# First tiles' masks on VectorE instead of bias products, zero products on TensorE, and a new written order, in a fused attention and tanh-shrink kernel

## The chip, the cores and the metric

The kernel runs on one core of a Trainium2 chip, in one launch. The metric is device time in microseconds. Five engines work side by side, each through its own queue in order: PE (TensorE, matrix products), ACT (ScalarE), DVE (VectorE), POOL (GpSimd) and SP (SyncE, here only DMAs). Three of them also issue DMAs; 16 DMA engines carry them out.

## What is computed

Attention with a few global keys and a local window, and then two matrix products with h - tanh(h) between them. B = 4, H = 8, S = 768, D = 64; 8 global keys, a window of 96; d_model 512, d_ff 2048.

```python
scores = scale * np.matmul(q, k.transpose(0, 1, 3, 2))
rel = pos[:, None] - pos[None, :]
is_global = pos[None, :] < n_global
is_local = (rel >= 0) & (rel < n_local)
keep = is_global | is_local
dist = np.where(is_global & ~is_local, n_local, np.abs(rel))
scores = np.where(keep, scores - slopes[:, None, None] * dist, -1e9)
a = softmax(scores)
x = np.matmul(a, v)      # heads side by side: 3072 rows of 512
h = x @ w_in
out = (h - np.tanh(h)) @ w_out
```

## The kernel before

The 3072 rows are 24 tiles of 128 query rows. `turn_of` puts the four tiles that begin a sequence first; these are tiles 0 to 3 in the kernel's own numbering. A tile has one block of 128 keys if it begins a sequence, and two otherwise (its own keys and those of the tile before, with the 8 global keys copied over the head of the older block where needed).

Every step has a short name, and the order in which the steps are put into the engines' queues is written out by hand in a string, `ORDER`. A second string, `HOMES`, says which buffer or which of the 8 PSUM banks each tile uses. An engine takes its own steps from `ORDER` one after the other; a step that has to wait holds up all that stands behind it on that engine. The steps of tile u:

- `lq.u`, `lk.u`, `lv.u`: loads of q, k and v. For tiles 0 to 2, q and k come as float32, q by ACT's queue and k by SP's (L294). From tile 3 on all loads are issued by POOL and converted on the way (L294 for tiles 3 and 4, L297 later), as are the weights `in.0` to `in.4` (parts of w_in, L300), `out.0` to `out.3` (quarters of w_out, L303) and most stores `st` (L454).
- `cq.u`, `ck.u`: conversion of the float32 rows to bf16, for tiles 0 to 2 (`/a` on ACT, `/d` on DVE).
- `T.u`: transposes. Up to tile 6 on PE (L317 for tiles 0 to 2, L321 for 3 and 4, L312 for 5 and 6), k first and then q; `Te.u.1` (k) and `Te.u.0` (q) copy them out of PSUM (L229 is ACT's copy, L231 DVE's). From tile 7 on, T is a DMA transpose on SP.
- `S.n`: products of keys and queries (L352). `E.u.o`: exponential on ACT (L359). `M.u.o`: the result times a mask on DVE (L363). `AV.u`: products with v and a column of ones (L378). `R.u`: reciprocal and division on DVE (L386, L387). `X.u`, `Xe.u`: transpose of x and its copy (L398).
- `m1.g.f`, `th.g.f`, `g.g.f`: the product with w_in for a group g of tiles (L420), tanh on ACT (L430), h - tanh(h) on DVE (L436). Tiles 0 and 1 are groups of one, tiles 2 to 7 groups of two, the rest groups of four. `m2.u.c.a`: the product with quarter a of w_out (L445), `ev.u` its copy out of PSUM.

The distance bias has two forms. For tile u >= `BIASED` (3 before), the mask `mk[m]` = exp(-slope * distance) is multiplied in after the exponential by step M. For tiles 0 to 2, step `B.u` has PE put the bias into the scores' PSUM banks first, by two products of 128x512 (L275), to which S adds; they have no step M. The masks themselves are made once, from the same kind of products (`bm.m`) and an exponential on ACT (`em.m`). Both rest on constants that DVE derives from `rel`, an iota that POOL makes first of all: `slopes`, `dist`, `first`; `turn` and `ident` are permutation and identity matrices for T and X.

The opening's queues before, as `ORDER` gives them:

```
PE   bm.1 bm.0 B.1 T.1 B.0 T.0 S.1 T.3 B.2 S.0 T.2 S.3 AV.0 S.2 AV.1 X.0 T.4 X.1 AV.2 bm.2 m1.0.0 AV.3 X.2 m1.1.0 X.3
     S.4 m1.2.0 m1.2.6 m1.1.4 ... m2.2.0.0 m1.2.4 m2.1.0.0 m2.0.0.0 m2.2.0.1
DVE  zero ones.0 slopes dist turn first ident ones.1 cq.1 ck.1 ck.0 Te.1.0 Te.0.0 ck.2 Te.3.0 Te.2.0 R.0 R.1 M.3.0 Te.4.1
ACT  lq.1 lq.0 lq.2 table em.1 em.0 cq.0 Te.1.1 Te.0.1 cq.2 E.1.0 Te.3.1 E.0.0 Te.2.1 E.3.0 E.2.0 Xe.0 Xe.1 Te.4.0 em.2
POOL rel lq.3 lk.3 lv.0 lq.4 lk.4 lv.1 lv.2 in.1 in.0 lv.3 in.2 lk.5 lq.5 in.3 out.0 out.1 out.2 lv.4 in.4 lk.6 lq.6
     lv.5 lq.10 lv.6 out.3
SP   lk.1 lk.0 lk.2
```

A function `warm()` with one product of zeros by zeros into bank 7 is there, but the order before does not call it.

Of the kernel before, what the change touches and what calls it, by code (L numbers as in the profile page):

```python
# [17 lines left out]
lq.1 lk.1 zero rel ones.0 lq.0 lk.0 lq.3 slopes lq.2 lk.2 lk.3 dist table lv.0 turn bm.1 first ident lq.4 ones.1 bm.0  # L18
em.1 lk.4 cq.1/d ck.1/d B.1 lv.1 em.0 T.1 lv.2 B.0 cq.0/a ck.0/d in.1 Te.1.0/d Te.1.1/a T.0 in.0 S.1 Te.0.1/a Te.0.0/d
cq.2/a ck.2/d E.1.0 lv.3 T.3 B.2 in.2 Te.3.1/a Te.3.0/d S.0 lk.5 T.2 E.0.0 lq.5 S.3 Te.2.0/d Te.2.1/a AV.0 in.3 R.0  # L20
E.3.0 S.2 AV.1 out.0 X.0 R.1 E.2.0 T.4 out.1 M.3.0 X.1 Xe.0/a AV.2 bm.2 Te.4.1/d Xe.1/a out.2 m1.0.0 R.2 Te.4.0/a em.2
lv.4 AV.3 X.2 R.3 m1.1.0 Xe.2/a X.3 th.0.0 S.4 Xe.3/d th.1.0 in.4 g.0.0 m1.2.0 E.4.0 lk.6 g.1.0 m1.2.6 K.4 E.4.1 M.4.0
lq.6 m1.1.4 th.2.0 M.4.1 m1.2.2 th.1.4 g.2.0 m1.0.4 th.2.6 g.1.4 lv.5 th.2.2 T.5 g.2.6 m1.1.8 th.0.4 Te.5.0/d Te.5.1/a
g.0.4 m1.0.8 th.1.8 g.2.2 lq.10 S.5 th.0.8 g.1.8 m1.2.10 E.5.1 g.0.8 m1.2.8 K.5 th.2.10 M.5.1 m2.2.0.0 lv.6 E.5.0
g.2.10 m1.2.4 th.2.8 M.5.0 m2.1.0.0 g.2.8 th.2.4 m2.0.0.0 g.2.4 out.3 m2.2.0.1 lk.8 m2.2.0.2 m2.0.0.1 AV.4 lq.7
m1.1.12 V.4 lk.10 R.4 m1.2.14 th.1.12 lq.8 m1.0.12 g.1.12 th.2.14 lk.9 g.2.14 m1.2.12 th.0.12 lk.7 m2.1.0.1 g.0.12
th.2.12 lq.9 X.4 g.2.12 AV.5 Xe.4/a m2.1.0.2 R.5 T.6 V.5 lv.7 m2.0.0.2 Te.6.1/a Te.6.0/d lk.11 X.5 m2.2.0.3 Xe.5/a
m2.0.0.3 ev.2.0/a T.10 S.6 ev.0.0/a m1.3.10 T.8 E.6.1 K.6 m1.3.0 E.6.0 M.6.1 T.7 m1.3.2 th.3.10 M.6.0 m2.3.0.0 T.9
th.3.2 g.3.10 m1.3.4 th.3.0 g.3.2 m2.1.0.3 g.3.0 th.3.4 AV.6 g.3.4 ev.1.0/a m1.3.6 R.6 st.1.0 m1.3.12 lv.15 th.3.6 V.6
m2.3.0.1 g.3.6 lq.12 th.3.12 S.7 g.3.12 lv.8 m2.3.0.2 E.7.1 K.7 lv.17 m1.3.8 E.7.0 lk.13 M.7.1 X.6 m2.3.0.3 Xe.6/d  # L30
lv.10 th.3.8 M.7.0 S.8 ev.3.0/a st.0.0 g.3.8 AV.7 lv.9 E.8.1 m1.3.14 V.7 R.7 lq.11 E.8.0 m2.4.0.0 M.8.1 lq.18 X.7
th.3.14 m2.4.0.1 M.8.0 lk.12 Xe.7/a S.9 g.3.14 lq.13 AV.8 E.9.1 K.9 m2.4.0.2 lq.15 R.8 E.9.0 m1.4.6 lv.11 M.9.1 Xe.8
m2.4.0.3 M.9.0 th.4.6 lv.12 T.11 m1.4.8 g.4.6 ev.4.0/a S.10 T.12 th.4.8 AV.9 E.10.1 K.10 g.4.8 m1.4.0 T.13 R.9 E.10.0
m2.5.0.0 M.10.1 Xe.9 m1.4.4 th.4.0 V.9 M.10.0 m1.4.10 th.4.4 g.4.0 m2.5.0.1 th.4.10 g.4.4 AV.10 lq.14 g.4.10 m2.5.0.2
R.10 lv.16 m1.4.2 V.10 lv.13 Xe.10 S.11 th.4.2 lk.15 m2.5.0.3 g.4.2 E.11.0 lk.14 K.11 m1.4.12 K.12 ev.5.0/d E.11.1
st.4.0 m1.4.14 M.11.0 lk.17 th.4.12 M.11.1 m2.6.0.0 th.4.14 st.5.0 g.4.12 m2.6.0.1 E.12.0 g.4.14 AV.11 M.12.0 m2.7.0.0
R.11 m2.7.0.1 V.11 Xe.11 S.12 m2.7.0.2 T.15 E.12.1 m2.7.0.3 E.13.1 M.12.1 T.14 m2.6.0.2 ev.7.0/d E.13.0 AV.12 M.13.1
st.7.0 m2.6.0.3 lq.16 M.13.0 m1.5.7 R.12 ev.6.0/a lv.14 m1.5.6 th.5.7 V.12 Xe.12 lk.16 m1.5.1 g.5.7 th.5.6 lq.17 AV.13
g.5.6 th.5.1 lv.18 m1.5.3 R.13 lq.23 m1.5.0 th.5.3 g.5.1 Xe.13 lk.18 m1.5.11 g.5.3 th.5.0 m1.5.8 g.5.0 lq.19 th.5.11
S.13 g.5.11 lk.19 th.5.8 m1.5.4 g.5.8 E.14.0 T.16 K.14 m1.5.2 K.15 E.14.1 M.14.0 T.17 m1.5.9 th.5.4 M.14.1 m1.5.13  # L40
th.5.2 g.5.4 m1.5.14 E.15.0 g.5.2 m1.5.10 th.5.13 M.15.0 th.5.14 m1.5.5 g.5.13 T.18 th.5.10 g.5.14 m2.8.0.0 th.5.5
g.5.10 m1.5.15 th.5.9 g.5.5 AV.14 th.5.15 g.5.9 m2.8.0.1 T.19 V.14 R.14 m1.5.12 m2.8.0.2 g.5.15 Xe.14 th.5.12 S.14
g.5.12 m2.9.0.0 E.15.1 K.16 m2.8.0.3 E.16.0 M.15.1 m2.9.0.1 ev.8.0/d E.16.1 AV.15 M.16.0 st.8.0 m2.10.0.0 lv.19 R.15
m2.9.0.2 lk.23 V.15 Xe.15 M.16.1 S.15 lv.22 m2.9.0.3 E.17.1 K.17 lv.23 m2.10.0.1 ev.9.0/d E.18.0 st.6.0 m2.10.0.2
M.17.1 lq.22 E.17.0 M.18.0 m2.10.0.3 st.3.0 st.2.0 M.17.0 AV.16 lv.21 m2.11.0.0 V.16 T.23 R.16 lv.20 AV.17 m2.11.0.1
R.17 st.9.0 Xe.16 ev.10.0/a m2.11.0.2 lk.20 V.17 Xe.17 m1.6.0 st.10.0 lq.21 S.16 th.6.0 lq.20 m2.11.0.3 g.6.0 E.19.1
K.19 lk.21 m1.6.9 ev.11.0/d E.19.0 m1.6.6 M.19.1 th.6.9 M.19.0 m1.6.4 th.6.6 g.6.9 m1.6.3 E.18.1 lk.22 g.6.6 m1.6.15
th.6.4 M.18.1 th.6.3 AV.19 g.6.4 AV.18 th.6.15 g.6.3 m1.6.12 R.18 m1.6.2 th.6.12 V.19 Xe.18 m1.6.8 g.6.15 th.6.2 R.19
m1.6.7 th.6.8 g.6.12 Xe.19 m1.6.1 th.6.7 g.6.8 m1.6.11 th.6.1 T.20 g.6.7 m1.6.5 th.6.11 g.6.1 T.21 m1.6.10 g.6.11
th.6.5 g.6.2 m1.6.14 th.6.10 T.22 g.6.5 m1.7.12 th.6.14 g.6.10 m1.6.13 th.7.12 g.6.14 m1.7.1 g.7.12 th.6.13 m1.7.10  # L50
g.6.13 th.7.1 S.17 g.7.1 th.7.10 m2.13.0.0 g.7.10 E.21.0 K.21 m2.12.0.0 K.20 E.20.0 M.21.0 m2.13.0.1 E.20.1 M.20.0
m2.12.0.1 M.20.1 m2.13.0.2 AV.20 m1.7.14 V.20 R.20 m2.13.0.3 th.7.14 Xe.20 m1.7.9 g.7.14 ev.13.0/a m2.12.0.2 th.7.9
m2.12.0.3 g.7.9 S.18 ev.12.0/a m1.7.5 E.21.1 K.22 m2.14.0.0 E.22.0 M.21.1 m1.7.3 th.7.5 M.22.0 m1.7.2 th.7.3 g.7.5
# [13 lines left out]
mk.0:2,3 mk.1:0,1 mk.2:6,7 f32.0.k:3 kq.0:1 f32.0.q:2 f32.1.k:1 kq.1:0 f32.1.q:0 f32.2.k:5 kq.2:3 f32.2.q:4 v.0:0
v.1:1 kq.3:2 v.2:2 kq.4:4 v.3:3 v.4:4 kq.5:0 v.5:5 kq.6:1 v.6:6 kq.7:4 v.7:7 kq.8:3 v.8:9 kq.9:0 v.9:4 kq.10:2 v.10:11
kq.11:1 v.11:5 kq.12:2 v.12:6 kq.13:3 v.13:7 kq.14:1 v.14:9 kq.15:0 v.15:8 kq.16:3 v.16:0 kq.17:2 v.17:10 kq.18:4
v.18:4 kq.19:1 v.19:11 kq.20:2 v.20:7 kq.21:4 v.21:6 kq.22:3 v.22:5 kq.23:0 v.23:1 tr.0.0:1 tr.0.1:7 qk.0:1 s.0.0:2,3  # L70
p.0.0:1 av.0:2,3 x.0:0 xt.0:2 xT.0:0 tr.1.0:6 tr.1.1:0 qk.1:0 s.1.0:4,5 p.1.0:0 av.1:4,5 x.1:1 xt.1:1 xT.1:1 tr.2.0:4
tr.2.1:5 qk.2:3 s.2.0:6,7 p.2.0:3 av.2:4,5 x.2:2 xt.2:3 xT.2:2 tr.3.0:0 tr.3.1:1 qk.3:2 s.3.0:0,1 p.3.0:2 av.3:0,1
x.3:0 xt.3:5 tr.4.0:3 tr.4.1:0 qk.4:4 s.4.0:6,7 s.4.1:0,1 p.4.0:4 p.4.1:1 av.4:0,1 x.4:1 xt.4:0 xT.3:3 tr.5.0:7
tr.5.1:3 qk.5:5 s.5.0:0,1 s.5.1:6,7 p.5.0:3 p.5.1:0 av.5:4,5 x.5:2 xt.5:0 tr.6.0:7 tr.6.1:1 qk.6:6 s.6.0:4,5 s.6.1:0,1
p.6.0:1 p.6.1:2 av.6:4,5 x.6:0 xt.6:3 xT.4:1 qk.7:9 s.7.0:6,7 s.7.1:4,5 p.7.0:0 p.7.1:4 av.7:2,3 x.7:1 xt.7:6 qk.8:8
s.8.0:4,5 s.8.1:6,7 p.8.0:1 p.8.1:3 av.8:6,7 x.8:2 xT.5:0 qk.9:10 s.9.0:2,3 s.9.1:4,5 p.9.0:0 p.9.1:2 av.9:0,1 x.9:0
qk.10:7 s.10.0:6,7 s.10.1:2,3 p.10.0:1 p.10.1:4 av.10:0,1 x.10:1 qk.11:4 p.11.0:3 p.11.1:0 av.11:2,3 x.11:2 qk.12:5
# [30 lines left out]
def kernel(  # L108
# [11 lines left out]
    nc = tc.nc  # L120

    B, H, S, Dh = q.shape
# [15 lines left out]
    R4 = 4  # L138

    ROWS = 5  # L140
    HW = 3
    PE_T = 7
    PE_X = 8
    BIASED = 3
    SINGLE = 2
    NK, NV, NQK = 5, 12, 11
    LAST = [(0, 384), (384, 512)]

    turn_of = sorted(range(NU), key=lambda t: (t % NQ > 0, t))
    nth = [t % NQ for t in turn_of]  # L150
# [438 lines left out]
```

## Time and profile before

| | us |
|---|---|
| median of three runs | 214.47 (213.91 to 216.38) |
| the profiled execution, its own time | 215.35 |
| its span, first to last instruction | 213.5 |
| busy: PE / DVE / ACT / POOL | 204.6 / 130.4 / 120.5 / 76.9 |
| L445, 400 products with w_out | 91.2 |
| L420, 576 products with w_in | 90.5 |
| L275, 12 bias products of 128x512 | 5.4 (mean 587 ns) |
| L359, 44 exponentials of 128x1024 | 43.0 (mean 1023 ns) |
| L363, 41 mask products of 128x1024 | 27.6 (mean 687 ns) |

The span is shorter than the time by what lies around it, 1.85 us. A line of the timeline has the start, the duration, the engine, the line of the code, the operation with what it writes and reads, how many of them are merged, and in brackets the idle time ahead with what ended it. Durations run from start to result; instructions of one engine overlap a little, so the step from one start to the next is often shorter. Twelve bias products are two each for three masks and three tiles.

### The profile page before, as it was taken

The numbers are of one execution on the slowest core, as the hardware profiler recorded it, in microseconds if no ns is written. First come the engines' busy times: TensorE is split into PE (matmuls) and PEld (weight loads), VectorE is DVE, ScalarE is ACT, GpSimd is POOL, SyncE is SP. The second block draws the span as 40 slices with busy tenths as digits, with TensorE's granted clock in tenths as the row PEclk, the third lists the DMA queues.
The fourth block names the chain that finished last, engine by engine and source line by source line (L and its number), as shares of the span: only waits on it lengthen the run. The fifth ranks groups of instructions, "written<-read, shape, count | busy, mean of one in ns | idle before, by whom it ended". The sixth has DMA issues, their size and how long they took to land.

```text
span 213.5 us, 4492 instructions
## 1 busy us (share of the span) xinstructions
PE 204.6 (96%) x1796; PEld 117.2 (55%) x1796; DVE 130.4 (61%) x264; ACT 120.5 (56%) x179; POOL 76.9 (36%) x101
## 2 busy tenths in 40 slices
PE   4799999999999999999999999999999999999994
PEld 1467985857667665544555454444554444444442
DVE  7348883737787975789776498874567435611300
ACT  4579881557678474578445395673853335522422
POOL 8794435730995092780049830000010002002040
PEclk9999999999999999999999999999999999999999
DMA  5999999999999999999919999801021102002136
GB/s 164 243 177 189 208 198 175 179 157 194 128 177 150 141 154 216 181 151 137 175 53 166 195 206 150 147 3 25 0 78 25 25 3 98 0 0 98 52 116 228
DMA packets 100884, 27.55 MB, mean 129 GB/s; under 512 B 91840, under 2 KB 99264, under 8 KB 100864
## 3 DMA queue, kind: packets, MB, share of 16 engines
q0 software_dynamic: 72000, 18.36, 85.1%
q1 hardware_dynamic: 28048, 8.13, 23.5%
q10 hardware_dynamic: 816, 0.79, 1.2%
q8 instruction: 14, 0.23, 0.4%
q14 instruction: 6, 0.05, 0.1%
HBM read 27.26 MB, written 6.29 MB: 157 GB/s over the span
## 4 chain that ended last, share of the span: by engine, by line
PE 68%; issue 12%; DMA 10%; POOL 6%; DVE 1%; ACT 0%; SPq 0%; POOLq 0%; DVEq 0%; ACTq 0%
PE ps L420 30%; PE ps L445 28%; DMA qk<-kq 4%; POOL kq L297 3%; PE ps L352 3%; DMA f<-in_k_dram 3%; PE ps L378 3%; DMA out_dram<-ot 3%; POOL vb L297 2%; PE ps L398 1%; PE ps L317 1%; POOL out_dram L454 1%; PE ps L321 1%; PE ps L275 1%; PE ps L312 0%
## 5 line engine op out<-in xcount | busy, mean ns | idle before, releaser
L445 PE MATMUL ps<-w_out_bf,g 128*128 128x512 bf16 (+2 forms) x400 | 91.2, 371 | 0.0
L420 PE MATMUL ps<-xT,w_in_bf 128*128 128x512 bf16 (+2 forms) x576 | 90.5, 308 | 0.5 <-ACT ot L229 0.5
L436 DVE TENSOR_TENSOR g<-ps,th 128x512 bf16<-128x512 f32 x96 | 65.0, 688 | 38.7 <-ACT th L430 37.5
L430 ACT ACTIVATE th<-ps 128x512 f32<-128x512 f32 x96 | 56.7, 599 | 45.6 <-PE ps L420 44.8
L420 PEld LDWEIGHTS <-w_in_bf 128*128 128x128 bf16 x576 | 50.2, 98 | 33.9 <-issue 0.8
L445 PEld LDWEIGHTS <-g 128*128 128x128 bf16 x400 | 37.0, 98 | 38.0 <-DVE g L436 0.5
L454 POOL DMA_DIRECT2D out_dram<-ot x21 | 12.0, 576 | 106.3 <-ACT ot L229 86.5
L359 ACT ACTIVATE pr<-ps 128x1024 bf16<-128x1024 f32 x44 | 43.0, 1023 | 9.8 <-PE ps L352 9.8
L363 DVE TENSOR_TENSOR pr<-pr,mk 128x1024 bf16<-128x1024 bf16 x41 | 27.6, 687 | 8.0 <-ACT pr L359 7.9
L229 ACT COPY ot<-ps 128x512 f32<-128x512 f32 (+2 forms) x20 | 11.3, 565 | 26.6 <-PE ps L445 19.2
L297 POOL DMA_DIRECT2D vb<-in_v_dram x24 | 21.7, 912 | 5.1 <-DMA w_out_bf<-in_moe_w_out_dram 2.6
L297 POOL DMA_DIRECT2D kq<-in_q_dram x19 | 17.1, 911 | 12.4 <-DMA qk<-kq 8.2
L297 POOL DMA_DIRECT2D kq<-in_k_dram x19 | 17.1, 903 | 1.2 <-PE ps L352 0.5
L387 DVE TENSOR_TENSOR x<-ps,rden 128x512 bf16<-128x512 f32 x24 | 16.6, 692 | 0.8
L378 PEld LDWEIGHTS <-pr 128*128 128x128 bf16 x352 | 13.5, 98 | 4.2 <-issue 0.2
L378 PE MATMUL ps<-vb,pr 128*128 128x65 bf16 x352 | 14.8, 194 | 0.0
L352 PEld LDWEIGHTS <-qk 64*128 64x128 bf16 x352 | 10.2, 96 | 7.0 <-issue 6.3
L352 PE MATMUL ps<-qk 64*128 64x128 bf16 x192 | 10.1, 229 | 0.0
L231 DVE COPY vb<-vb 8x512 bf16<-8x512 bf16 x16 | 5.7, 356 | 5.9 <-PE ps L378 5.9
L275 PE MATMUL ps<-slopes,dist 128*128 128x512 bf16 x12 | 5.4, 587 | 3.1 <-DVE dist L242 3.1
L352 PE MATMUL ps<-qk,qk 64*128 64x128 bf16 x160 | 7.8, 217 | 0.0
L386 DVE RECIPROCAL rden<-ps 128x8 f32<-128x8 f32 x24 | 4.8, 199 | 2.8 <-PE ps L378 2.6
(41 smaller groups left out, 58.8 us busy)
## 6 DMA issues: line engine op xcount, KB each, us to landing
out_dram<-ot POOLq DMA_DIRECT2D x21, 256.0 KB, 2.8
vb<-in_v_dram POOLq DMA_DIRECT2D x24, 128.0 KB, 6.1
kq<-in_q_dram POOLq DMA_DIRECT2D x21, 128.0 KB, 6.9
kq<-in_k_dram POOLq DMA_DIRECT2D x21, 128.0 KB, 7.5
w_out_bf<-in_moe_w_out_dram POOLq DMA_DIRECT2D x4, 512.0 KB, 13.1
w_in_bf<-in_moe_w_in_dram POOLq DMA_DIRECT2D x3, 512.0 KB, 10.5
f<-in_q_dram ACTq DMA_DIRECT2D x3, 256.0 KB, 4.2
f<-in_k_dram SPq DMA_DIRECT2D x3, 256.0 KB, 6.9
```

What stands on the lines that cost most here:

```text
L229: nc.scalar.copy(out=out, in_=in_)
L297: eng(e).dma_start(out=dst, in_=rows_of(src, u).rearrange("h p d -> p h d"))
L352: nc.tensor.matmul(bank(("s", u, o), hh)[:, p * P : (p + 1) * P], buf(("qk", back[u] if o else u))[r, 1, p, :], buf(("qk", u))[r, 0, p, :] ...
L359: nc.scalar.activation(d, banks(("s", u, o), 0, 1), AF.Exp, bias=0.0, scale=scale)
L363: nc.vector.tensor_tensor(out=t, in0=t, in1=mk[:, mask_of(u, o)], op=ALU.mult)
L378: nc.tensor.matmul(t[:, h // (H // 2), h % (H // 2), :], buf(("p", u, o))[:, slot(h), :], buf(("v", back[u] if o else u))[:, h, 0 : Dh + 1 ...
L387: nc.vector.tensor_tensor(out=buf(("x", u)).rearrange("q (a h) d -> q a h d", a=2), in0=t[:, :, :, 0:Dh], in1=rden.to_broadcast([P, 2, H / ...
L420: nc.tensor.matmul(t[:, (f - f0) * n : (f - f0 + 1) * n], w_in_bf[j][:, c, fo : fo + P], x[:, c, 0:n], start=(c == 0), stop=(c == CD - 1),)
L430: nc.scalar.activation(h_view(buf(("th", g, f0)), g, m), h_view(bank(("h", g, f0)), g, m), AF.Tanh, bias=0.0, scale=1.0)
L436: nc.vector.tensor_tensor(out=buf(("g", g))[:, f0 : f0 + m, 0:n], in0=h_view(bank(("h", g, f0)), g, m), in1=h_view(buf(("th", g, f0)), g, ...
L445: nc.tensor.matmul(bank(part)[:, 0 : c1 - c0], buf(("g", g))[:, f, t * P : (t + 1) * P], w_out_bf[f // FJ][:, f % FJ, c0:c1], start=(f == ...
L454: eng(e).dma_start(out=out[turn_of[u] * P : (turn_of[u] + 1) * P, c0:c1], in_=buf(("ot", u))[:, c0:c1])
```

## The change

`BIASED` goes from 3 to 0: steps B.0, B.1 and B.2 with their six products are gone, S starts the sum itself, and tiles 0, 1 and 2 get a step M (M.0.0, M.1.0, M.2.0). The order may hold words `zero:b`, each one product of 128x512 of zeros into bank b; sixteen are in it. `ORDER` and `HOMES` are written anew from end to end.

```diff
-    BIASED = 3
+    BIASED = 0
...
-    def warm():
-        nc.tensor.matmul(ps[:, 7, :], zero[:, 0, :], zero.to_broadcast([P, 4, P]), start=True, stop=True)
+    def warm(b):
+        nc.tensor.matmul(ps[:, b, :], zero[:, 0, :], zero.to_broadcast([P, 4, P]), start=True, stop=True)
...
-            if word == "warm":
-                warm()
+            if word.startswith("zero:"):
+                warm(int(word[5:]))
                 continue
```

The opening's queues after:

```
PE   zero:7 zero:7 zero:7 zero:7 bm.1 bm.0 zero:7 T.1 zero:7 zero:7 T.0 S.1 zero:6 S.0 zero:7 zero:7 T.2 T.3 zero:1 zero:3
     AV.1 S.2 AV.0 S.3 X.1 zero:1 zero:1 zero:1 zero:3 AV.2 X.0 AV.3 bm.2 m1.1.0 X.2 X.3 m1.0.0 m1.2.2 m1.2.4 m1.1.4 m1.2.6
     T.4 m1.2.8 m1.0.4 S.4 m1.2.10 m1.0.12 m1.2.14 m1.2.12 AV.4 T.5 m1.2.0 m1.1.8 m1.1.12 S.5 m2.1.0.0 T.6 m1.0.8 m2.0.0.0
     m2.2.0.0 m2.2.0.1
DVE  zero ones.0 slopes turn dist ident first ones.1 cq.1 ck.1 ck.0 Te.1.1 Te.0.0 cq.2 ck.2 M.1.0 Te.2.1 M.0.0 R.1 R.0
     M.2.0 M.3.0 R.2 R.3 Xe.2 Xe.3
ACT  lq.1 lq.0 lq.2 table em.1 em.0 cq.0 Te.1.0 Te.0.1 E.1.0 E.0.0 Te.2.0 Te.3.0 Te.3.1 E.2.0 E.3.0 Xe.1 Xe.0 em.2 th.1.0
POOL rel lk.3 lq.3 lv.2 lv.1 lv.0 in.0 lv.3 in.1 lq.4 in.2 lk.4 in.3 in.4 lq.5 lk.5 lk.7 lv.4 lq.6 out.0 lk.6 lv.5 out.1
     out.2 out.3
SP   lk.1 lk.0 lk.2
```

The masks' products `bm.0` to `bm.2`, the arithmetic of all other steps and the number of loads and stores are as before.

## The prediction

> **What bounds it now.** I read the page's busy table first, then PE's waits, then the opening.
>
> ```profile
> PE 204.6 (96%) x1796; PEld 117.2 (55%) x1796; DVE 130.4 (61%) x264; ACT 120.5 (56%) x179; POOL 76.9 (36%) x101
> ```
> ```profile
> PE ps L420 <- ACT ot L229: 0.5, 1, 0.5
> ```
>
> The second line is all that PE waited for after 20 us. From there to 210.4 it runs without a gap, so nothing there can get faster by a new order, apart from that 0.5. The page's chain wanders through DMA and POOL between 67 and 119, but PE is full there too. What can shrink is the opening (and the 3.1 us tail, which keeps its shape: last products, two copies, two stores). In windows of 3.41 us (columns: busy PE, weight load, DVE, ACT, POOL, clock, DMA):
>
> ```profile
> 1.77:5.18 3.41, 2.07 (x5) 0.70 (x6) 2.93 (x25) 2.28 (x3) 3.41 (x5) 1.00 0.84 247
> 5.18:8.60 3.42, 2.38 (x12) 1.11 (x10) 0.31 (x2) 1.93 (x4) 2.94 (x5) 1.00 1.19 276
> 8.60:12.01 3.41, 2.72 (x33) 2.19 (x34) 2.12 (x4) 2.39 (x4) 2.31 (x3) 1.00 1.96 177
> 12.01:15.42 3.41, 3.41 (x34) 1.92 (x32) 1.38 (x2) 2.05 (x4) 3.26 (x4) 1.00 1.68 186
> ```
>
> PE's timeline shows the path and a change of speed:
>
> ```profile
> 8.97 1.04 PE L317 MATMUL ps<-turn,kq 128*128 128x128 bf16 x8 [1.42 <-DVE kq L231]
> ...
> 10.87 1.06 PE L321 MATMUL ps<-turn,kq 128*64 128x128 bf16 x16 [0.32 <-DVE qk L231]
> 11.86 1.03 PE L275 MATMUL ps<-slopes,dist 128*128 128x512 bf16 x2
> 12.83 0.61 PE L352 MATMUL ps<-qk 64*128 64x128 bf16 x8
> 13.37 1.03 PE L317 MATMUL ps<-turn,kq 128*128 128x128 bf16 x8
> 14.34 0.61 PE L352 MATMUL ps<-qk 64*128 64x128 bf16 x8
> 14.88 0.62 PE L378 MATMUL ps<-vb,pr 128*128 128x65 bf16 x8
> 15.43 0.40 PE L352 MATMUL ps<-qk 64*128 64x128 bf16 x8
> ...
> 16.92 0.64 PE L321 MATMUL ps<-turn,kq 128*64 128x128 bf16 x16
> 17.49 0.40 PE L398 MATMUL ps<-ident,x 128*128 128x128 bf16 x4
> 17.72 0.41 PE L378 MATMUL ps<-vb,pr 128*128 128x65 bf16 x8
> 17.97 0.59 PE L275 MATMUL ps<-slopes,dist 128*128 128x512 bf16 x2
> ```
>
> T.0 (8.97) starts when DVE has cast tile 0's k, landed at 8.46. The same sixteen products (L321) step on after 0.99 us at 10.87 and 0.57 at 16.92: until about 15.4 PE runs at half speed, though the clock column says 1.00 throughout. PE had worked unbroken for 4.55 us (10.87 to 15.42) when it sped up; the 4.45 us from 3.11 to 7.56 had not brought T.0 to full speed.
>
> **The change, part by part.** *Bias products.* Six of 128x512 go. Four (at 3.11 and 6.50) lie where PE waits for loads: worth nothing, but they were what kept PE busy. B.2's two at 11.86 are on the path: 0.97 us.
>
> *Masks.* M.0.0, M.1.0, M.2.0 come to DVE: 0.60 us of its queue each (M.3.0 at 17.29 to the next at 17.89), and 0.68 plus a hop of 0.05 between E and AV. AV.1 gets this for nothing (PE is at T.2, T.3). Queued behind M.1.0 and M.0.0 are Te.2.1, R.1 and R.0; behind M.2.0, M.3.0 and R.2.
>
> *Turn before dist, ident before first:* dist 0.22 later; bm.1 goes from 3.11 to 3.33. Casts of tile 1 wait for the same DVE queue, T.1 still stands at about 5.5, and everything waits for 8.46 anyway: nothing. (rel leads GpSimd's queue in both, so "distances first" moves nothing here.)
>
> *Zero products.* Sixteen, 0.43 each at half speed (B.2's two take 0.97 with their change-over), 0.22 at full (bm.2: 0.43 for two). Four before bm.1 (about 1.0 to 2.7), one before T.1, two after it: PE is then busy 3.33 to 7.3, 4.0 us, less than the stretch that had no visible effect. Seven lie in idle time. The five from zero:6 to zero:3 lie where PE is on the path or close to it. From T.0 on they leave no gap: by the 4.55 us above, PE is at full speed at 8.97+4.55=13.5.
>
> The Trainium skill, "TensorE: Matmul & The Clock Gate", Part 1, has a free-running window of about 3.4 us that must be busy once. The trace fits that (2.72 busy of 3.41 was not enough, 3.41 was). By this rule the change of speed would fall anywhere from 12.4 to 15.8 (an estimate), or, if a window falls into the 4.0 us, before T.0, and differ between runs; the first lies about my 13.5, the second is the third rival.
>
> *Walk of the new order from T.0,* with each row's duration; loads as before, speed changing at 13.5. PE: T.0 8.97, S.1 9.94, zero to 10.91, S.0 10.91 (12.83 before), two zeros to 12.31 (T.2 could start at 11.55, ck.2 being done: they cost 0.76), T.2 to 13.28, T.3 to 13.96, two zeros to 14.39, AV.1, S.2 14.63, AV.0, S.3 15.28. ACT (0.92 per E, 0.48 per copy): E.1 10.6, E.0 11.56, Te.2.0 13.4, Te.3.0 14.17, Te.3.1 14.65, E.2 15.13, E.3 16.05, Xe.1 16.97, Xe.0 17.45. DVE (0.61 per mask or copy, R 0.23+0.61): M.0.0 13.56, R.1 14.9, R.0 15.74, M.2.0 16.58, M.3.0 to 17.88. PE: X.1 15.88, four zeros to 16.97 (hidden, AV.2 waits for M.2.0), AV.2 17.32, X.0, AV.3 17.93, bm.2, m1.1.0 18.6, X.2, X.3, m1.0.0 19.91, m1.2.2 20.78. Before, m1.2.0 starts at 21.75 with S.4 (0.55) and T.4 (0.57) done, which the new order has yet to do: 20.78+1.12-21.75 = +0.15. B.2's 0.97 and the half-speed time won are spent on zeros ahead of T.2, the masks and ACT, which gets E.2 no sooner than 15.1 (14.98 for E.3 before).
>
> *The queue of loads.* On POOL lv.2, lv.1, lv.0 pass lq.4 and lk.4 (T.4 now comes 4 us into the dense part), in.3 and in.4 pass the w_out parts, and lq.5, lk.5, lk.7, lv.4, lq.6 come ahead of out.0. w_out, then, is later:
>
> ```profile
> 29.84 0.88 POOL L297 DMA_DIRECT2D vb<-in_v_dram  x1 [1.18 <-DMA w_out_bf<-in_moe_w_out_dram]
> ```
>
> Issue n waits for landing n-8 (the ninth waits for the first at 8.5), so this one, the 24th, says that out.1, 16th, landed at 29.8; likewise out.2 32.3, in.4 36.0. Now out.0 is 19th and out.1 22nd. By bytes out.1 then lands at 36.0 (5.0 MB, as much as up to in.4 before); by packet time about 38.7 (the trace's packets last 34 ns at 128 bytes, 60 at 512, 98 at 1,024; over 16 engines a tile of q, k or v, 1,024 packets, is 2.2 us, a w_out part 3.1; out.1 closes 47.4 us of them, in.4 before 41.8 at 36.0, out.3 before 55.9 at 42.9). PE reaches m2.1.0.0 at 20.78+13.9=34.7 (13 m1 of 0.87, 2.6 of S, T, AV) and m2.2.0.1 at 38.6: just covered, so 0. Uncovered it is the second rival.
>
> *The rest of the order.* It has the same products. The 0.5 at 119.5 (a copy that waited for a store) may go, or others come: 0 to -0.5 against some +1; I take 0.
>
> Sum: 215.35 (profiled execution: 213.5 and 1.85 around it) +0.15 = 215.5. The median of the three runs is 0.9 below that execution; as the change of speed may well have come earlier in them, I carry half: **215.1**.
>
> **Rivals.** *The speed changes late (15.4, as before).* The walk with half speed until then has two zeros to 15.13, S.2 15.55, E.3 to 17.95, m1.1.0 19.49, m1.2.2 21.71: +1.08, **216.4**, slower at the edge of what counts. It is also what happens if zero products do nothing for the speed. Against: 4.55 us of unbroken work were enough once.
>
> *w_out late: slower.* If the queue goes on at the 0.71 us per us of packet time that it kept from 20.2 to 36.0, out.1 (5.6 us of packets after in.4's place) lands at about 39.9 and m2.2.0.1 waits 1.3: 215.5+1.3, **216.8**; each further us of landing or a like wait of a later tile adds one. It decides from a landing at 39.7. For: PE never waited for loads here before, with only 1.5 us to spare for in.4 (36.0 against 37.5). Against: the ring is filled sooner.
>
> *Full speed before T.0: faster.* Then T.0 is through at 9.5, E.1 starts 10.0, E.2 13.3, m1.1.0 16.8 (in.1 lands about then), m1.2.2 19.02: -1.6, **213.7**, 213.2 without the 0.5 at 119.5, and 212.3 if the runs lie 0.9 lower as before. For: PE busy from 1.0 with 0.6 us of gap. Against: 4.45 us at the same place did not do it.
>
> **Numbers.** Bounds: 1% is about what runs of this kernel (213.9 to 216.4) can tell; 212.3 and 216.6 are the borders. Forecast 0.40 (within); late speed 0.13 (0.07 slower, 0.06 within); w_out or a like load late 0.25 (slower); early speed 0.22 (0.14 faster, 0.08 within). So faster 0.14, within 0.54, slower 0.32. The range runs from early speed at 212.4 to w_out one us later still, 217.6; the likeliest case alone 214.2 to 216.2.
>
> **What would show it.** L321's sixteen products near 13.3 in about 0.7 us, later ones in 0.57; S.0 at 10.9; PE idle before T.2 none; m1.1.0 at 18.6; no wait of L445 for w_out at 34 to 40; M between E and AV. I am wrong if lk.0 lands elsewhere than 8.5, if T.3 is slow (first rival) or T.0 fast (third), or if PE has gaps after 20 us.

## The result and the profile after

| | before | after |
|---|---|---|
| median of 20 runs each, us | 214.58 (213.32 to 217.17) | 215.68 (213.95 to 217.41) |
| ratio of the times | | 1.0049, 95% interval [1.0027, 1.0071] |
| the profiled execution, its own time | 215.35 | 215.69 |
| its span | 213.5 | 213.4 |
| what lies around the span | 1.85 | 2.29 (median of the 20 runs) |

Medians here and below are of all runs; ratios and their intervals leave out the few runs that were counted as slow.

The change made the kernel slower by half a per cent, which is inside the 1% that was called no difference. The profile after, however, has an opening that is far better than forecast. First, PE's timeline of the opening (start, duration, engine, line, operation, count, idle time ahead and what ended it; line numbers are one higher than before, so L421 is m1, L446 m2, L353 S, L318 and L322 T; L542 is the zero products):

```profile
5.53 0.97 PE L318 MATMUL ps<-turn,kq 128*128 128x128 bf16 x8
6.34 0.59 PE L542 MATMUL ps<-zero 128*128 128x512 bf16 x2
8.04 0.62 PE L318 MATMUL ps<-turn,kq 128*128 128x128 bf16 x8 [1.11 <-DVE kq L232]
...
9.44 0.40 PE L353 MATMUL ps<-qk 64*128 64x128 bf16 x8
9.77 0.61 PE L542 MATMUL ps<-zero 128*128 128x512 bf16 x2
10.21 0.61 PE L318 MATMUL ps<-turn,kq 128*128 128x128 bf16 x8
10.75 0.64 PE L322 MATMUL ps<-turn,kq 128*64 128x128 bf16 x16
...
15.95 1.06 PE L421 MATMUL ps<-xT,w_in_bf 128*128 128x128 bf16 x16
...
17.29 1.93 PE L421 MATMUL ps<-xT,w_in_bf 128*128 128x128 bf16 x24
19.57 1.61 PE L421 MATMUL ps<-xT,w_in_bf 128*128 128x256 bf16 x18 [0.35 <-DMA w_in_bf<-in_moe_w_in_dram]
```

T.0 takes 0.62 us where it took 1.04: PE is at full speed already, from 6.30 on (T.1, which runs across that moment, takes 0.97, the two zeros right behind it 0.59). Tile 0's k also came 1.2 us earlier than in the profile of before (its cast on DVE starts at 7.29, not 8.49; T.0 at 8.04, not 8.97). The first product with w_in is at 15.95. The last eight of the 24 at 17.29 are m1.2.2; they start near 18.18. When the kernel before starts m1.2.0, at 21.75, it has S.4 and T.4 done as well, which take 1.12; with these the new kernel would stand at 19.30. So PE enters the dense part 2.45 us ahead, and yet the span is shorter by 0.1 only. This compares one execution of each kernel: the one of before, at 215.35, lies 0.77 above its median, and half speed lasted until 15.42 in it, so between the medians the lead may well be smaller. The dense part has given nearly all of it back. Its waits, in the list of PE's waits (total, times, longest) of the kernel after:

```profile
PE ps L353 <- DMA qk<-kq: 1.0, 2, 0.6
...
PE ps L421 <- DMA xT<-x: 0.6, 1, 0.6
...
PE ps L421 <- DMA w_in_bf<-in_moe_w_in_dram: 0.3, 1, 0.3
```

Before, the only wait of the dense part was the 0.5 for a copy. All of these are for transfers: a part of w_in, two DMA transposes of q and k, one of x. The timeline shows three of them with the products ahead:

```profile
54.28 0.81 PE L446 MATMUL ps<-w_out_bf,g 128*128 128x512 bf16 x3
55.52 0.40 PE L353 MATMUL ps<-qk 64*128 64x128 bf16 x8 [0.43 <-DMA qk<-kq]
...
85.83 0.81 PE L446 MATMUL ps<-w_out_bf,g 128*128 128x512 bf16 x3
87.29 1.47 PE L421 MATMUL ps<-xT,w_in_bf 128*128 128x512 bf16 x6 [0.65 <-DMA xT<-x]
...
105.65 0.40 PE L353 MATMUL ps<-qk,qk 64*128 64x128 bf16 x8
106.65 0.40 PE L353 MATMUL ps<-qk 64*128 64x128 bf16 x8 [0.60 <-DMA qk<-kq]
```

By the step from one start to the next, less what that step takes without a wait, they cost 0.59, 0.81 and 0.79, and the one for w_in, behind the product that starts at 18.95, costs 0.51: 2.7 in all, against 0.64 before (the 0.5 for a copy). Of 2.45 won, 2.06 are gone by these, and the last product ends 0.17 earlier than before (210.20 against 210.37); some 0.2 are not traced. Then come 0.44 us around the span that before does not have.

What the waits for q and k stand behind shows in the issues of the DMA transposes on SP. The lines give the time an issue takes, minimum, median and largest in ns, the first and last start in us, and the time to landing; first before, from 40 to 57 us, then after:

```profile
L333 SPq DMA_TRANSPOSE qk<-kq x4: 1242/1296/3403, 45.1 to 51.5; - x4
...
DMA to landing us min/median/max: 3.1/4.3/6.1
```
```profile
L334 SPq DMA_TRANSPOSE qk<-kq x3: 2023/2487/2961, 43.2 to 48.5; - x3
...
DMA to landing us min/median/max: 9.0/9.5/10.1
```

They start 2 us earlier, but take 9 to 10 us to land, not 3 to 6: the trace has the three down at 52.2, 55.5 and 58.0, the four of before at 51.1, 52.0, 53.4 and 54.5. In these microseconds POOL issues five loads of q, k and v (41.9 to 47.2), which land up to 58.4; before, it issued none between 43.98 and 54.07, and the last of the earlier ones was down at 50.1. Even there the two transposes issued ahead of that moment took 6.1 and 5.4 us, the two behind it 3.3 and 3.1. So the new order has the transposes and the loads side by side, and what PE needs next is no earlier. That the loads are what slows the transposes is argued from these rows; no run moves the loads alone.

### The profile page after: what moved, and what is told of

It is laid out like the page before. It is cut to its first block, busy times and chain, and to the rows that moved or that the text cites. A ratio compares the mean times of both kernels' runs of the same rounds, so it can differ in the third digit from the quotient of the medians.

```text
span 213.4 us, 4495 instructions
## 1 busy us (share of the span) xinstructions
PE 203.7 (95%) x1780; PEld 116.3 (54%) x1806; DVE 130.4 (61%) x265; ACT 122.1 (57%) x181; POOL 76.9 (36%) x101
## 4 chain that ended last, share of the span: by engine, by line
PE 77%; DMA 19%; issue 1%; POOL 1%; DVE 0%; ACT 0%; POOLq 0%
PE ps L421 34%; PE ps L446 33%; DMA qk<-kq 9%; DMA w_in_bf<-in_moe_w_in_dram 5%; PE ps L353 5%; PE ps L379 4%; DMA kq<-in_q_dram 3%; DMA xT<-x 3%; POOL kq L295 1%; PE ps L313 0%; DVE x L388 0%; PE ps L399 0%; PE ps L322 0%; POOL rel L236 0%; ACT ot L230 0%
## 5 line engine op out<-in xcount | busy, mean ns | idle before, releaser
L421 PE MATMUL ps<-xT,w_in_bf 128*128 128x512 bf16 (+2 forms) x572 | 89.9, 308 | 1.3 <-DMA xT<-x 0.6
L446 PE MATMUL ps<-w_out_bf,g 128*128 128x512 bf16 (+2 forms) x379 | 87.1, 370 | 1.4 <-issue 0.5
L421 PEld LDWEIGHTS <-w_in_bf 128*128 128x128 bf16 x576 | 50.0, 98 | 34.4 <-DMA xT<-x 1.1
L446 PEld LDWEIGHTS <-g 128*128 128x128 bf16 x400 | 36.9, 98 | 39.1
L364 DVE TENSOR_TENSOR pr<-pr,mk 128x1024 bf16<-128x1024 bf16 x44 | 29.9, 688 | 8.7 <-ACT pr L360 8.2
L230 ACT COPY ot<-ps 128x512 f32<-128x512 f32 (+2 forms) x21 | 11.9, 566 | 20.7 <-PE ps L446 17.4
L379 PEld LDWEIGHTS <-pr 128*128 128x128 bf16 x352 | 13.5, 97 | 5.0 <-DVE pr L364 0.8
L353 PEld LDWEIGHTS <-qk 64*128 64x128 bf16 x352 | 10.0, 94 | 7.0 <-issue 4.2
L353 PE MATMUL ps<-qk 64*128 64x128 bf16 x192 | 9.5, 218 | 1.1 <-DMA qk<-kq 1.0
L353 PE MATMUL ps<-qk,qk 64*128 64x128 bf16 x160 | 7.8, 217 | 0.0
L230 ACT COPY xT<-ps 128x512 bf16<-128x512 bf16 x6 | 3.5, 587 | 6.8 <-PE ps L399 6.8
L542 PE MATMUL ps<-zero 128*128 128x512 bf16 x16 | 5.7, 458 | 1.0 <-DVE zero L463 1.0
```

The source lines that it names most:

```text
L230: nc.scalar.copy(out=out, in_=in_)
L353: nc.tensor.matmul(bank(("s", u, o), hh)[:, p * P : (p + 1) * P], buf(("qk", back[u] if o else u))[r, 1, p, :], buf(("qk", u))[r, 0, p, :] ...
L364: nc.vector.tensor_tensor(out=t, in0=t, in1=mk[:, mask_of(u, o)], op=ALU.mult)
L379: nc.tensor.matmul(t[:, h // (H // 2), h % (H // 2), :], buf(("p", u, o))[:, slot(h), :], buf(("v", back[u] if o else u))[:, h, 0 : Dh + 1 ...
L421: nc.tensor.matmul(t[:, (f - f0) * n : (f - f0 + 1) * n], w_in_bf[j][:, c, fo : fo + P], x[:, c, 0:n], start=(c == 0), stop=(c == CD - 1),)
L446: nc.tensor.matmul(bank(part)[:, 0 : c1 - c0], buf(("g", g))[:, f, t * P : (t + 1) * P], w_out_bf[f // FJ][:, f % FJ, c0:c1], start=(f == ...
```

## The experiments

All times are medians of runs that alternate with runs of the kernel before on the same chip; ratios are to those.

**The opening made late again** (x1): eight zero products more, which hold up PE between AV.3 and bm.2 and nothing else.

```diff
-AV.3 bm.2 lk.7 m1.1.0
+AV.3 zero:4 zero:4 zero:4 zero:4 zero:4 zero:4 zero:4 zero:4 bm.2 lk.7 m1.1.0
```

> The changed kernel with eight more zero products just before bm.2, about 1.7 us of PE's path at full speed (they go into bank 4, which is free there). In the profile of the changed kernel m1.1.0 starts at 15.95, and PE then waits in four places for transfers: for in.2 at 19.6, for T.7 at 55.5, for a transposed x at 87.3 and for q and k of a tile at 106.7, 2.0 us in all by the list of waits. Theory A (what the opening gains is given back at these transfers, which stand where the queue of loads lets them): m1.1.0 at about 17.7, the four waits together under 1.0, time 0 to 0.7 us above the changed kernel. Theory B (the waits belong to the new order and move with it): the waits stay at about 2, time 1.7 above the changed kernel, ratio to the kernel before about 1.013.

217.89 us, 1.0118 [1.0056, 1.018] (few runs). The delay came out larger than the 1.7 us meant, so the time lies above both ranges, and the waits have to decide: in this execution T.0 started at 9.55, and a stretch from 10.68 to 14.10 ran at half speed besides:

```profile
9.55 0.62 PE L318 MATMUL ps<-turn,kq 128*128 128x128 bf16 x8 [2.29 <-DVE kq L232]
...
12.33 1.06 PE L318 MATMUL ps<-turn,kq 128*128 128x128 bf16 x8
...
18.44 1.89 PE L542 MATMUL ps<-zero 128*128 128x512 bf16 x8
20.38 0.38 PE L276 MATMUL ps<-slopes,dist 128*128 128x512 bf16 x1
20.59 1.06 PE L421 MATMUL ps<-xT,w_in_bf 128*128 128x128 bf16 x16
```

m1.1.0 is 4.64 us later than after, but the span grew by 1.9 only (215.3 against 213.4): 2.7 went unseen, as much as the waits for transfers come to. And these are gone; the list of PE's waits holds none for a DMA. The transposes themselves did not move:

```profile
L334 SPq DMA_TRANSPOSE qk<-kq x3: 1337/3057/4296, 43.3 to 48.3; - x3
...
DMA to landing us min/median/max: 9.4/9.9/10.2
```

They start at 43.3 and land 9.4 to 10.2 us later, as after, with PE 4.64 us later. The first of them waits for the load of the q that it turns, and that load lands at 43.19 here and at 43.10 after. Product by product, the lead of the kernel after over x1 falls from 4.64 to 4.13 at its wait for w_in (19.57), to 3.6 at 55.52, to 2.71 at 87.29 and to 1.82 behind 106.65, and stays there to the end. This is the main reading: in the dense part of the new order, transfers set a pace that an earlier opening does not change.

**The zeros taken out** (x2), nothing else changed.

```diff
-zero:7 zero:7 T.0 ... zero:6 ... zero:7 ... zero:7 ... zero:1 zero:3
+T.0
```

> The changed kernel without its sixteen zero products. If the zero products bring PE to full speed before T.0 (profile of the changed kernel: eight products of T.0 in 0.62 us): here T.0 takes about 1.04, full speed comes between 12 and 16 us, and m1.1.0 starts 1 to 2.5 us after 15.95. Theory A: the waits after 19 us shrink to under 1.0 and the time is within 0.7 us of the changed kernel. Theory B: time 1 to 2.5 us above it. If the zero products do nothing: T.0 as fast as with them, m1.1.0 no later, time up to 0.7 lower.

216.64 us, 1.0096 [1.0057, 1.0136]. In its profiled execution, 1.3 us above that median, T.0 ran in 1.03 us at 9.34, PE stayed at half speed to about 21, m1.1.0 came at 19.61, and PE waited for no transpose and no part of w_in. By the medians the zeros are worth about 1 us to the change (216.64 against 215.68); the two intervals overlap, and 0.96 falls between the ranges of the two theories, so this run alone doesn't decide between them.

**The masks alone** (x3): the kernel before with its order, six bias products out, M.0.0, M.1.0 and M.2.0 behind their exponentials.

```diff
-    BIASED = 3
+    BIASED = 0
```

> The kernel before with the bias products of tiles 0 to 2 replaced by masks on DVE, and nothing else moved (no zero products, old order). If B.2's 0.97 us on the path is what the masks save and the masks are hidden: m1.0.0 starts 0.5 to 1.0 us before 18.4 where full speed comes at the same time, time 0 to 0.8 below the kernel before. If the masks take the path instead (0.7 each between exponential and AV): time 0 to 0.8 above. PE is less busy ahead of T.0 (two products fewer from 4.8 and two from 6.5), so full speed before T.0 should not come more often than in the kernel before.

215.96 us, 1.0065 [1.0033, 1.0097]: a little slower. AV.0 and AV.2 of the old order come too soon for the masks (the idle time ahead in brackets):

```profile
15.25 0.62 PE L378 MATMUL ps<-vb,pr 128*128 128x65 bf16 x8 [0.84 <-DVE pr L363]
...
19.26 0.42 PE L378 MATMUL ps<-vb,pr 128*128 128x65 bf16 x8 [0.39 <-DVE pr L363]
```

Full speed was reached near 18.4 in this execution and m1.0.0 started at 19.95, not 18.40. So in the old order the 0.97 us of B.2 on the path are not saved: the masks put 1.23 there. The longer half speed may come from less work on PE or from where the stretches of the clock fell in this execution; the run doesn't part the two, and so not how much of the 0.65% is the masks' own.

**Zeros alone** (x4): the kernel before with four zero products ahead of bm.1.

```diff
-lq.1 lk.1 zero rel ones.0
+lq.1 lk.1 zero zero:7 zero:7 zero:7 zero:7 rel ones.0
```

> The kernel before with four zero products ahead of bm.1 and nothing else changed. PE is then busy from 1.0 to 7.6 but for about 0.4. If that brings full speed before T.0: eight products of T.0 in 0.6, m1.0.0 1.5 to 2.5 us before 18.4. Theory A: the old order gives part of it back at its loads, time 0 to 1.0 below the kernel before, with PE waits after 20 us above the 0.5 of before. Theory B: no new waits, time 1.5 to 2.5 below, ratio about 0.990. If zero products do not count for the speed: T.0 in 1.04 as before and the time unchanged.

214.66 us, 1.0009 [0.9968, 1.0049]: nothing. The windows of its profile (busy time of PE, weight load, DVE, ACT, POOL with counts; granted clock; DMA share; GB/s) say why:

```profile
6.45:9.87 3.42, 1.62 (x21) 0.85 (x18) 1.45 (x3) 1.82 (x4) 2.28 (x3) 1.00 1.44 238
9.87:13.28 3.41, 2.60 (x30) 1.73 (x32) 1.39 (x3) 2.10 (x4) 2.51 (x3) 0.50 1.96 173
13.28:16.69 3.41, 3.41 (x44) 2.38 (x44) 2.06 (x5) 3.23 (x4) 3.12 (x5) 0.50 1.67 188
16.69:20.11 3.42, 3.37 (x69) 3.09 (x71) 2.99 (x7) 3.02 (x5) 1.62 (x2) 1.00 1.65 188
```

Full speed was there for T.0 (0.62), but PE waited 1.64 us for it, was busy 1.62 of the 3.42 us, and lost the speed for the next 6.83. The products ahead of T.0 raise the speed; the gap ahead of T.0 takes it away again. The four zeros had no part in raising it here: they end at 2.89, and the stretch that brought full speed is 3.04 to 6.45 (3.34 us busy), where PE does what it does in the kernel before. That it was filled here and not there is chance, by where the stretches fell. The kernel before gets full speed and loses it again in many runs: 16 of the 29 that alternate with x1 to x4 have a mean granted clock of 0.983 to 0.992 (x4's profiled execution: 0.984).

**The gap filled, old order** (y3) **and new order** (y4): eight zero products ahead of T.0, in the kernel before (with the four of x4) and in the kernel after.

```diff
-T.0
+zero:7 zero:7 zero:7 zero:7 zero:7 zero:7 zero:7 zero:7 T.0
```

> The kernel before with four zero products ahead of bm.1 and eight more just ahead of T.0, so that PE has no gap from 3.1 until T.0's k has landed. With four alone the profile shows full speed at 6.4, half speed again from 9.8 (after a gap of 1.6 us) and full speed from 16.6. Theory S (the speed falls back because of the gap before T.0, and that is what zero products have to fill): granted clock 1.00 in nearly all runs, T.0 in 0.6 and everything after it at full speed, m1.0.0 at 16 to 17, no new waits after 20 us, span near 211.2, time 1 to 2 us below the kernel before, ratio 0.991 to 0.996. If the speed falls back all the same, or if eight products hold up T.0: ratio 0.998 to 1.003.

> The changed kernel with eight more zero products just ahead of T.0, where PE is idle from 6.9 to 8 or 9.5. Theory S: granted clock 1.00 in nearly all runs and m1.1.0 near 16. Theory A (what the opening gains is given back at the transfers): the PE waits after 19 us are 2 to 3 in all, the span stays near 212.5 to 213 and the time is no more than 0.8 below the changed kernel. If the new order's dense part could use an early opening: 1 to 2.5 us below it.

| | time, us | ratio to before | span, median | around it |
|---|---|---|---|---|
| y3, old order | 214.33 | 0.9982 [0.9944, 1.0019] | 212.45 | 1.86 |
| y4, new order | 215.45 | 1.0034 [1.0004, 1.0065] | 213.2 | 2.25 |

In none of the 24 runs did the speed fall back (mean granted clock of at least 0.997; x4 has runs of 0.984). So the gap is what the zeros have to fill. y3's time was to fall by 1 to 2 us with that and did not. Its opening, in its timeline:

```profile
6.98 1.89 PE L541 MATMUL ps<-zero 128*128 128x512 bf16 x8
9.34 0.62 PE L317 MATMUL ps<-turn,kq 128*128 128x128 bf16 x8 [0.47 <-DVE kq L231]
...
16.79 1.07 PE L420 MATMUL ps<-xT,w_in_bf 128*128 128x128 bf16 x16
```

m1.0.0 is at 16.79 with T.0 at 9.34, where x4 had 18.11 with T.0 at 8.72. But the spans of the two profiled executions are 212.6 and 212.7: the old order hands its early opening back too. These are in y3's list of PE's waits, and not in x4's:

```profile
PE ps L420 <- DMA w_in_bf<-in_moe_w_in_dram: 0.5, 1, 0.5
...
PE ps L352 <- DMA qk<-kq: 0.3, 1, 0.3
```

The first ends at 36.45, the second at 75.48; y3's lead over x4 falls there from 1.3 to 0.58 and from 0.58 to 0.18.

At equal speed the old order is 1.12 us ahead of the new one by the medians, 0.75 of it in the span. The profiled executions of y3 and y4 have the same span, 212.6, so no trace shows where the 0.75 lies. In y4 the opening is as early as after (m1.1.0 at 15.88), and its list of waits has it back in one place (with 0.3 for w_in it waits for 1.6 in all, less than the 2 to 3 of theory A):

```profile
PE ps L421 <- DMA xT<-x: 1.3, 1, 1.3
```

**Bias products in the new order** (y1): B.0 to B.2 in place of five of the zeros, M.0.0 to M.2.0 out; then the same with the eight zeros ahead of T.0 (z2), beside y4 with three copies moved from DVE to ACT (z1, below).

```diff
-    BIASED = 0
+    BIASED = 3
...
-T.1 lv.3 cq.0/a zero:7 ck.0/d in.1 zero:7 Te.1.1/d
+T.1 lv.3 cq.0/a B.1 ck.0/d in.1 Te.1.1/d
```

> The changed kernel with tiles 0 to 2 biased on PE again: B.1 in place of the two zero products before T.0, B.0 in place of zero:6, B.2 in place of zero:1 and zero:3 ahead of AV.1; M.0.0, M.1.0 and M.2.0 are gone. PE's filling is as long as before, so the difference is the masks. Theory M (masks cost path time: in the old order the masks alone made the kernel 0.65% slower, with AV waiting 0.84 and 0.39 for them): AV.1, AV.0 and AV.2 start 0.3 to 0.7 earlier, the time is 0.5 to 1.5 us below the changed kernel, ratio to the kernel before 0.998 to 1.003. Rival (the masks alone lost through a later full speed, PE being less busy, and not through their own time): no difference from the changed kernel, ratio about 1.005.

> The changed kernel with tiles 0 to 2 biased on PE again (y1_after_bias_back) and eight zero products ahead of T.0, so that it can be set beside y4_after_zeros_to_T0 with the speed the same: granted clock 1.00 in both. Theory A (the opening's gain or loss is absorbed at the transfers): span 212.8 to 213.5 as in y4_after_zeros_to_T0 (213.2), whether the masks are on PE or DVE; time about 0.4 below it, all of it around the span (262 on DVE). Theory M (masks cost path time that reaches the end): span 0.5 to 1.0 below 213.2.

y1: 215.87 us, 1.006 [1.0023, 1.0096]. z2: 215.14 us, 1.0032 [1.0003, 1.0062], span 213.35. With the masks (y4) the ratio was 1.0034 and the span 213.2: in the new order it makes no measurable difference which engine applies the bias of the first tiles. The 0.5 to 1.5 us that theory M gave to y1 did not come, and z2 came out as theory A had it. z2 waits for a transfer like the others, in yet another place:

```profile
PE ps L353 <- DMA qk<-kq: 1.1, 1, 1.1
```

**The time around the span** (y2, z1). y2 issues the stores of three more tiles on SP instead of POOL; z1 is y4 with `ev.7`, `ev.8` and `ev.13` on ACT, so that DVE has no more instructions than before.

```diff
-POOL if u < NU - 3 else SP
+POOL if u < NU - 6 else SP
```
```diff
-ev.7.0/d ... ev.8.0/d ... ev.13.0/d
+ev.7.0/a ... ev.8.0/a ... ev.13.0/a
```

> The changed kernel with the stores of tiles 18, 19 and 20 issued by SP instead of POOL; nothing else. The time around the span is 2.29 us (median of 20 runs) against 1.86 for the kernel before, where POOL's last store is issued at 207.4 and not at 208.8. If POOL's late stores make the end: 1.9 around the span, time 0.4 below the changed kernel. If it is something else in the order: 2.3 again and the time unchanged.

> The changed kernel with the eight added zero products ahead of T.0 (the run named y4_after_zeros_to_T0), and three copies out of PSUM (ev.7, ev.8, ev.13) given to ACT instead of DVE: DVE has 262 instructions in place of 265. So far every kernel whose page has 265 or more on DVE fetched one more 8 KB block of code about 2 us after the span's end, and had 2.0 to 2.35 us around the span; those with 264 or fewer had none and 1.77 to 1.86. Theory C (the masks push DVE's code over the edge of a block): no such block, about 1.85 around the span, time 0.4 below y4_after_zeros_to_T0. Rival (what lies around the span comes with the order of the end): 2.25 again and the same time.

y2: 215.34 us, 1.0034 [0.9998, 1.007], 2.26 around the span as after. POOL's stores at the end are not it. z1: 215.36 us, 1.0038 [1.0008, 1.0067]; the time around the span fell to 1.78, but the median span was 213.55 and not 213.2, and the time stayed. So with three copies fewer on DVE the 0.4 is gone, as theory C says and its rival doesn't. All kernels fit that: with 262 instructions on DVE the time around the span is 1.77 to 1.78 (y1, z1, z2), with 264 it is 1.84 to 1.91 (before, x4, y3, z3), with 265 to 268 it is 1.99 to 2.35 (after, x1, x2, x3, y2, y4, w1). The late block of code, which was to be the mechanism, fits less well: z1's trace has it too, 1.0 us behind the end of the span, and z3's 1.8 behind, where the kernels with 265 and more have it 1.6 to 2.1 behind; z2's has none. How the count makes the 0.4 is open.

**A still earlier opening of the old order** (z3): tile 1's scores and exponential ahead of T.0, in.1 and in.0 ahead of lq.4, lk.4 and lv.2.

```diff
-B.1 lv.1 em.0 T.1 lv.2 B.0 cq.0/a ck.0/d in.1 Te.1.0/d Te.1.1/a T.0 in.0 S.1
+B.1 in.0 em.0 T.1 B.0 Te.1.1/a Te.1.0/d cq.0/a ck.0/d zero:7 zero:7 S.1 E.1.0 zero:7 zero:7 ... T.0
```

> The kernel before with zero products up to T.0 (y3_before_zeros_to_T0, whose profile has m1.0.0 at 16.8, waiting 0.5 for in.0), and in its opening tile 1 no longer behind tile 0: Te.1 ahead of tile 0's casts, S.1 and E.1.0 ahead of T.0, S.0 ahead of T.3, in.1 and in.0 loaded ahead of lq.4, lk.4 and lv.2, T.4 after AV.2. If the opening still decides with the old dense order: m1.0.0 at 15.0 to 16.0, no wait for in.0, span 0.5 to 1.2 below the 212.45 of y3_before_zeros_to_T0, ratio 0.990 to 0.996. If the old order too hands it back at its transfers: waits after 19 us of 1 us and more, span 212 to 212.5, ratio 0.997 to 0.999.

215.07 us, 1.0044 [1.0007, 1.0082]: a miss, above both ranges. (The 0.5 that the expectation puts at in.0 is y3's wait at 36.45, for a later part of w_in.) In the profiled execution, 217.81, lv.2, now later in POOL's queue, made AV.2 wait 0.91 us, and the speed fell back once more at 17.56.

**The new opening ahead of the old dense part** (w1): up to m1.0.0 the order of y4 (without in.3, in.4, lq.5, lk.5, lk.7 and lv.4), then the old order, with T.4 and S.4 ahead of m1.2.0.

```diff
 m1.1.0 R.3 em.2 X.2 X.3 th.1.0 Xe.2/d m1.0.0
-Xe.3/d g.1.0 m1.2.2 th.0.0 lq.6 g.0.0 m1.2.4
+lk.5 lq.5 in.3 out.0 T.4 out.1 Xe.3/d Te.4.1/d out.2 Te.4.0/a lv.4 th.0.0 g.1.0 g.0.0 in.4 S.4 E.4.0 m1.2.0
```

> The opening of the changed kernel (masks by VectorE, no bias products, zero products and the eight more ahead of T.0, up to the first m1 of tile 0), followed by the old order of the dense part with its old loads; no tile has a bias product. If it is the new order behind the opening, by the places of its transfers, that costs: no wait for a transfer over 0.4 us after 20 us, m1.2.0 at about 19 to 20.5, the span at 211.5 to 212.6 (the old order with zeros ahead of T.0: 212.45; the new one: 213.2) and the time at 213.8 to 214.8, ratio 0.995 to 1.000. If it is the masks or the new opening themselves: span about 213.2, time about 215.4, ratio 1.003. If any order hands an early opening back at its transfers: waits for loads or DMA transposes of 1 to 2.5 us appear after 20 us, and the ratio is 0.999 to 1.002.

217.33 us, 1.0104 [1.0069, 1.0138], slower than either order whole, and above all three expectations. The seam is bad: lk.4 stands later in the new opening's queue than the old dense part needs it. PE's timeline and windows there, in a profiled execution 2 us above the median (five of the nine runs have its mean granted clock of 0.992, one stretch at half speed):

```profile
20.19 0.64 PE L322 MATMUL ps<-turn,kq 128*64 128x128 bf16 x16 [0.45 <-DMA kq<-in_k_dram]
21.50 0.40 PE L353 MATMUL ps<-qk 64*128 64x128 bf16 x8 [0.68 <-ACT qk L230]
```
```profile
19.52:22.94 3.42, 1.87 (x38) 1.34 (x36) 2.04 (x4) 2.07 (x4) 3.04 (x4) 1.00 1.62 192
22.94:26.35 3.41, 3.41 (x20) 2.54 (x18) 2.08 (x3) 1.53 (x3) 1.22 (x2) 0.50 1.26 212
```

The waits for T.4's load and for the copy behind it come to over 1 us; they drop PE's busy time to 1.87 of 3.42, and the next stretch runs at half speed, 1.7 us more; later PE waits 1.5 us for a transpose of x, as it did in y4. So of the three expectations the last is nearest (an early opening handed back at transfers, in the old dense order too, at least behind this queue of loads), but the seam is large enough that the run does not part the other two. y3 shows the handing back in the old order without a seam.

## Why the prediction was right, and where it was not

The time was forecast at 215.1 and came at 215.68, within 1% of before, as the likeliest case said. But the profiled execution did not go the likeliest case's way. Full speed came ahead of T.0, and early speed with a time within the 1% had a chance of 0.08. The number was right by two terms that were both off and cancelled, and that is luck.

- *The sum.* For the profiled execution it gave 215.5, and 215.69 was measured. The step to 215.1, half of the 0.9 by which the three runs lay below the profiled one, did not hold: with 20 runs the median of before is 214.58, and after's median is equal to its profiled execution.
- *The opening, +0.15.* Mis-sized: it was -2.45 between the two profiled executions. Its premise was that the zeros ahead of T.0 would not bring full speed before 13.5 and that m1.1.0 would come at 18.6. In the profiled run it is the third rival that took place: full speed at 6.30, m1.1.0 at 15.95 (16.8 in the rival), m1.2.2 at 18.18 (19.02). The step "busy 3.33 to 7.3, less than the stretch that had no visible effect" failed: what matters is how full one stretch of 3.41 us is. The 4.45 us of before lay across two of them (2.07 and 2.38 us busy, the first two windows that the prediction shows), and after one had 3.06 (2.89 to 6.30); x4 shows that the kernel before can fill one as well. That the stretches lie differently from run to run was said; that the speed can be lost again, as in x1, y1 and y2, was not. Tile 0's k landing elsewhere than at 8.5, one of the signs of being wrong, came too: T.0 starts 0.93 earlier by it.
- *That early speed means faster.* This is where the third rival's price failed: it gave 213.7 and assumed that what the opening wins stays won. The 2.45 us were handed back at transfers.
- *The rest of the order, 0.* Wrong by 2.06: the wait of 0.5 for a copy went, and 2.7 of waits for transfers came. "0 to -0.5 against some +1" had named them, and too small. x1 shows that they are there only when PE is early, so with a slow opening the zero would have been about right.
- *w_out late.* Did not happen; PE never waited for L446's weights. Its reasoning, a queue of loads that lands at a pace of its own, held for another member of that queue: in.2 held up PE until 19.57. Later it was the transposes on SP, which the prediction had nowhere in its sum.
- *Masks hidden on DVE.* Held for the new order (y4 and z2), where they lie beside other work as walked. In the old order the same masks (x3) cost 0.65%, in part by waits of 1.23 us for them. The 0.97 us of B.2 can't be booked as a saving.
- *Around the span.* Taken as 1.85; it is 2.29. The sum had no term for a change of it. It goes with the number of instructions on DVE (z1); the mechanism is open.

Of the 1.1 us between the medians, some 0.6 are in the span (212.7 to 213.0 in the runs of before beside the experiments, 213.4 after) and 0.4 around it.

What stays open besides: whether another order of the loads and transposes would let the new dense order keep its early start (w1 tried only an old one, with a bad seam), why the old order is 0.75 us shorter in the span at equal speed, and why tile 0's k lands anywhere between a start of T.0 at 7.98 and one at 10.02, in kernels that issue that load alike.

## What to carry to other kernels

An opening made faster by 2 us is worth that only if the transfers that the steady part waits for move with it. Look at when the next transfers are issued and land, not at whether PE waits for them now: a wait of zero says nothing of how much earlier it could start. If zero products are to hold the speed, they belong where PE would otherwise wait long, directly ahead of the first product on the path, since speed gained earlier is lost in the gap. What that saved here is not clear of the noise (y3: 0.9982, interval up to 1.0019).

## What was unexpected of the hardware

The granted clock of this core is set in stretches of 3.413 us (its changes lie 3.41 us apart in x1, 6.83 in x4 and 10.24 in z3), at phases that differ from run to run. In six of the profiled executions it fell to half within the span, and each time the stretch ahead had PE busy for no more than 1.87 us of 3.41 (1.12, 1.18, 1.59, 1.62, 1.77 and 1.87: x1, y1, y2, x4, z3, w1). The kernel after kept full speed through a stretch with 2.21:

```profile
2.89:6.30 3.41, 3.06 (x13) 1.33 (x14) 2.00 (x18) 3.19 (x4) 3.41 (x5) 1.00 1.11 304
6.30:9.71 3.41, 2.21 (x30) 1.22 (x27) 2.30 (x5) 2.17 (x4) 2.94 (x5) 1.00 1.57 258
```

At half speed, stretches of 2.60 (x4), 2.72 (before), 2.80 and 2.94 (x2) did not bring full speed; all of 3.05 and more did (3.05 in y2, y4 and w1, 3.06 after, 3.12 in z2). Products of zeros count as work for this: in y4 they fill 2.3 us of the stretch from 5.14 to 8.55, all of which is busy and which kept full speed. In a single execution the column can read 1.00 for time at half speed, where no change was recorded yet, as in the profile of before up to 15.42; the step between starts tells.

The Trainium skill, "TensorE: Matmul & The Clock Gate", Part 1, puts the window at 3413 ns and calls it free-running, and the runs agree. That part of the Trainium skill also asks for about one whole idle window before the clock falls, and here the measurement differs: stretches with 1.12 to 1.87 us of work were followed by half speed, and in x4 a single wait of 1.64 us was enough (1.62 of 3.42 busy).

Between 40 and 57 us, DMA transposes took 9.0 to 10.1 us from issue to landing in the kernel after, where POOL issued loads beside them, and 3.1 to 6.1 in the kernel before, where it issued none. Their issue on SP also took longer, 2.5 us in the median instead of 1.3.
